# RMSNorm: VectorE's share of the squares moved to ScalarE, which reads x through PSUM copies made by TensorE

## Chip, cores and metric

One core of a Trainium2 chip. The metric is the device time of one execution in microseconds (us); smaller is better. Quoted times are medians of several runs with the lowest and highest in brackets. Runs of the slow state (here: over 1.5% longer than the fastest run of the same kernel) are named where there are any and are left out of every ratio.

Names of the engines in the profile: PE is TensorE's matmul, PEld its weight load, DVE is VectorE, ACT is ScalarE, POOL is GpSimd, SP is SyncE. SBUF and PSUM are the two on-chip memories that the kernel uses: its loads land in SBUF, its matmuls write to PSUM.

## The reference

```python
B, S, D = 512, 32, 640            # x: bf16 [512, 32, 640], g: bf16 [640]
def reference(x, g):
    rms = jnp.sqrt((x * x).mean(axis=-1, keepdims=True) + 1e-6)
    return x / rms * g
```

There are 16384 rows of 640 elements, so each of the 128 partitions holds 128 rows. "A row" below is one row on each of the 128 partitions, a 128x640 operand. The kernel works in 19 chunks, c0 to c18, of 2, 4, 4, fourteen times 8, 4 and 2 rows.

## The kernel before

For each chunk: one load, the mean square of each row (on ACT or on DVE), one square root on ACT, one reciprocal on DVE, one scaling per row on DVE, one product with g on DVE, one store. The parts that matter:

```python
DVE_SS_EVERY = float(os.environ.get("K_DVE_EVERY", "6"))   # every 6th row's square is DVE's
FRONT = [...  "2,2,2" ...]                                 # DVE squares in c0, c1, c2
IO_BUFS = 6; O_BUFS = 3; NODVE_LAST = 3                    # (defaults, shortened)
# ... (cut: pools, g broadcast by a ones-matmul) ...
    for ci, J in enumerate(sizes):
        x_sb_full = xin_pool.tile([P, JM, D], xf.dtype)
        x_sb = x_sb_full[:, :J, :]
        in_eng.dma_start(out=x_sb, in_=x_v[:, r0:r0 + J, :])
        # ... (cut: n_dve, the number of this chunk's squares that DVE takes; na = J - n_dve)
        for j in range(J):
            if j >= na:
                nc.vector.scalar_tensor_tensor(out=junk_d[:], in0=x_sb[:, j, :], scalar=inv_d,
                    in1=x_sb[:, j, :], op0=ALU.mult, op1=ALU.mult, accum_out=ms[:, j:j + 1])
            else:
                nc.scalar.activation(out=junk_a[:], in_=x_sb[:, j, :], func=ACT.Square,
                    scale=inv_sqrt_d, accum_out=ms[:, j:j + 1])
        # ... (cut: tiles; scale_rows and finish, called one after the other)
            nc.scalar.activation(out=rstd[:, j0:j1], in_=ms[:, j0:j1], func=ACT.Sqrt, ...)
            nc.vector.reciprocal(out=rstd[:, j0:j1], in_=rstd[:, j0:j1])
            for j in range(j0, j1):
                nc.vector.tensor_scalar_mul(out=o_sb[:, j, :], in0=src[:, j, :], scalar1=rstd[:, j:j + 1])
            nc.vector.tensor_tensor(out=o_sb, in0=o_sb, in1=g_bcast(J), op=ALU.mult)
            out_eng.dma_start(out=o_v[:, r0:r0 + J, :], in_=o_sb)   # last three chunks: nc.sync
```

Semaphores, and the order of instructions on each engine, are set by the framework when the program is built; each engine then works through its own queue in that order (ACT's late roots in e_psum_dve6, below, show it).

Of the kernel before, what the change touches and what calls it, by code (L numbers as in the profile page):

```python
# [11 lines left out]
J_MAX = int(os.environ.get("K_J", "8"))  # L12
RAMP = [int(v) for v in os.environ.get("K_RAMP", "2,4").split(",") if v]
DRAMP = [int(v) for v in os.environ.get("K_DRAMP", "4,2").split(",") if v]
DVE_SS_EVERY = float(os.environ.get("K_DVE_EVERY", "6"))
FRONT = [int(v) for v in os.environ.get("K_FRONT", "2,2,2").split(",") if v]
IO_BUFS = int(os.environ.get("K_BUFS", "6"))
O_BUFS = int(os.environ.get("K_OBUFS", "3"))
S_BUFS = int(os.environ.get("K_SBUFS", "4"))
OUT_ENG = os.environ.get("K_OUTENG", "gpsimd")  # L20
IN_ENG = os.environ.get("K_INENG", "sync")
G_ENG = os.environ.get("K_GENG", "sync")
G_AFTER = int(os.environ.get("K_GAFTER", "0"))
WARM_SQRT = int(os.environ.get("K_WARM", "1"))
SPLIT = int(os.environ.get("K_SPLIT", "0"))
LAG = int(os.environ.get("K_LAG", "1"))
TTFIRST = int(os.environ.get("K_TTFIRST", "0"))
NODVE_LAST = int(os.environ.get("K_NODVE_LAST", "3"))
LASTOUT_SYNC = int(os.environ.get("K_LASTOUT_SYNC", "3"))
NOLAG_LAST = int(os.environ.get("K_NOLAG_LAST", "0"))  # L30


def chunk_schedule(R):
    start = list(RAMP)
    end = list(DRAMP)
    rem = R - sum(start) - sum(end)
    assert rem >= 0
    mid = []
    while rem >= J_MAX:
        mid.append(J_MAX)  # L40
        rem -= J_MAX
    if rem:
        mid = [rem] + mid
    sizes = start + mid + end
    assert sum(sizes) == R
    return sizes
# [3 lines left out]
def kernel(  # L50
# [6 lines left out]
    nc = tc.nc  # L57
    P = nc.NUM_PARTITIONS
    ALU = mybir.AluOpType
    ACT = mybir.ActivationFunctionType  # L60
    f32 = mybir.dt.float32
# [2 lines left out]
    xf = x.flatten_outer_dims()  # L64
    of = out.flatten_outer_dims()
    N, D = xf.shape
    assert N % P == 0
    R = N // P

    x_v = xf.rearrange("(p r) d -> p r d", p=P)  # L70
# [1 line left out]

    sizes = chunk_schedule(R)
    JM = max(sizes)

    consts = ctx.enter_context(tc.tile_pool(name="consts", bufs=1))
    xin_pool = ctx.enter_context(tc.tile_pool(name="xin", bufs=IO_BUFS))
    out_pool = ctx.enter_context(tc.tile_pool(name="xout", bufs=O_BUFS))
    junk_pool = ctx.enter_context(tc.tile_pool(name="junk", bufs=2))
    small = ctx.enter_context(tc.tile_pool(name="small", bufs=S_BUFS))  # L80
    PACC = int(os.environ.get("K_PACC", "0"))
    if PACC:
        pacc_pool = ctx.enter_context(tc.tile_pool(name="pacc", bufs=PACC, space=bass.MemoryType.PSUM))
    PJUNK = int(os.environ.get("K_PJUNK", "0"))
    if PJUNK:
        pjunk_pool = ctx.enter_context(tc.tile_pool(name="pjunk", bufs=PJUNK, space=bass.MemoryType.PSUM))

    engines = {"sync": nc.sync, "scalar": nc.scalar, "gpsimd": nc.gpsimd, "vector": nc.vector}
    in_eng = engines[IN_ENG]
    out_eng = engines[OUT_ENG]  # L90

    eps_sb = consts.tile([P, 1], f32)
    nc.vector.memset(eps_sb[:], EPS)  # L93
# [4 lines left out]
        warm2 = consts.tile([P, 1], f32)  # L98
        nc.scalar.activation(out=warm2[:], in_=warm[:], func=ACT.Sqrt, bias=eps_sb[:], scale=1.0)  # L99

    GBC = os.environ.get("K_GBC", "pe_act")
    g_sb = consts.tile([P, D], g.dtype)
    g_src = bass.AP(tensor=g.tensor, offset=g.offset, ap=[[0, P], g.ap[-1]])
    if GBC == "dma":
        if not G_AFTER:
            engines[G_ENG].dma_start(out=g_sb[:], in_=g_src)
    else:
        g1 = consts.tile([1, D], g.dtype)
        g_row = bass.AP(tensor=g.tensor, offset=g.offset, ap=[[0, 1], g.ap[-1]])
        engines[G_ENG].dma_start(out=g1[:], in_=g_row)  # L110
        ones1 = consts.tile([1, P], bf16)
        nc.vector.memset(ones1[:], 1.0)  # L112
        gps_pool = ctx.enter_context(tc.tile_pool(name="gps", bufs=1, space=bass.MemoryType.PSUM))
        half = D // 2
        for h in range(2):
            gp = gps_pool.tile([P, half], f32, name=f"gp{h}")
            nc.tensor.matmul(out=gp[:], lhsT=ones1[:], rhs=g1[:, h * half:(h + 1) * half],  # L117
                             start=True, stop=True)
            if GBC == "pe_act":
                nc.scalar.copy(out=g_sb[:, h * half:(h + 1) * half], in_=gp[:])  # L120
            else:
                nc.vector.tensor_copy(out=g_sb[:, h * half:(h + 1) * half], in_=gp[:])

    inv_sqrt_d = 1.0 / float(D) ** 0.5
    inv_d = 1.0 / float(D)

    def g_bcast(J):
        return bass.AP(tensor=g_sb.tensor, offset=g_sb.offset,
                       ap=[list(g_sb.ap[0]), [0, J], list(g_sb.ap[-1])])

    gidx = 0
    r0 = 0
    pending = []
    for ci, J in enumerate(sizes):
        x_sb_full = xin_pool.tile([P, JM, D], xf.dtype)
        x_sb = x_sb_full[:, :J, :]
        in_eng.dma_start(out=x_sb, in_=x_v[:, r0:r0 + J, :])
        if G_AFTER and ci == 0:
            engines[G_ENG].dma_start(out=g_sb[:], in_=g_src)

        if ci < len(FRONT):
            n_dve = min(J, FRONT[ci])
        elif NODVE_LAST and ci >= len(sizes) - NODVE_LAST:
            n_dve = 0
        else:
            n_dve = 0
            for j in range(J):
                k = gidx + j
                if DVE_SS_EVERY and (int(k // DVE_SS_EVERY) != int((k + 1) // DVE_SS_EVERY)):
                    n_dve += 1  # L150
        na = J - n_dve

        if PACC:
            ms = pacc_pool.tile([P, JM], f32)
        else:
            ms = small.tile([P, JM], f32)
        for j in range(J):
            if j >= na:
                junk_d = junk_pool.tile([P, D], bf16)
                nc.vector.scalar_tensor_tensor(  # L160
                    out=junk_d[:],
                    in0=x_sb[:, j, :],
                    scalar=inv_d,
                    in1=x_sb[:, j, :],
                    op0=ALU.mult,
                    op1=ALU.mult,
                    accum_out=ms[:, j:j + 1],
                )
            else:
                if PJUNK:  # L170
                    junk_a = pjunk_pool.tile([P, D], f32)
                else:
                    junk_a = junk_pool.tile([P, D], bf16)
                nc.scalar.activation(  # L174
                    out=junk_a[:],
                    in_=x_sb[:, j, :],
                    func=ACT.Square,
                    scale=inv_sqrt_d,
                    accum_out=ms[:, j:j + 1],
                )  # L180

        rstd = small.tile([P, JM], f32)
        o_sb_full = out_pool.tile([P, JM, D], of.dtype)
        o_sb = o_sb_full[:, :J, :]
        if TTFIRST:
            nc.vector.tensor_tensor(out=o_sb, in0=x_sb, in1=g_bcast(J), op=ALU.mult)

        def scale_rows(j0, j1, rstd=rstd, ms=ms, x_sb=x_sb, o_sb=o_sb):
            if j1 <= j0:
                return  # L190
            nc.scalar.activation(out=rstd[:, j0:j1], in_=ms[:, j0:j1], func=ACT.Sqrt,  # L191
                                 bias=eps_sb[:], scale=1.0)
            nc.vector.reciprocal(out=rstd[:, j0:j1], in_=rstd[:, j0:j1])  # L193
            for j in range(j0, j1):
                src = o_sb if TTFIRST else x_sb
                nc.vector.tensor_scalar_mul(out=o_sb[:, j, :], in0=src[:, j, :],  # L196
                                            scalar1=rstd[:, j:j + 1])

        def finish(J=J, o_sb=o_sb, r0=r0, ci=ci):
            if not TTFIRST:  # L200
                nc.vector.tensor_tensor(out=o_sb, in0=o_sb, in1=g_bcast(J), op=ALU.mult)  # L201
            if LASTOUT_SYNC and ci >= len(sizes) - LASTOUT_SYNC:
                nc.sync.dma_start(out=o_v[:, r0:r0 + J, :], in_=o_sb)
            else:
                out_eng.dma_start(out=o_v[:, r0:r0 + J, :], in_=o_sb)  # L205

        if SPLIT and 0 < n_dve:
            scale_rows(0, na)

            def tail(J=J, na=na, scale_rows=scale_rows, finish=finish):  # L210
                scale_rows(na, J)
                finish()

            pending.append(tail)
        else:
            scale_rows(0, J)
            if SPLIT:
                pending.append(finish)
            else:
                finish()  # L220
        lag = LAG if ci < len(sizes) - NOLAG_LAST else 0
        while len(pending) > lag:
            pending.pop(0)()

        r0 += J
        gidx += J
    while pending:
        pending.pop(0)()


# [28 lines left out]
```

## Time and profile before

| | before |
|---|---|
| time, us | 113.94 (113.86 to 114.06, 3 runs) |
| span of the profiled run, us | 112.0 |
| DVE busy / ACT busy / PE busy | 92% / 73% / 1% |
| DMA rate while loads and stores both run | about 427 GB/s |

The span is the part of a run that the trace covers; the reported time is some 1.9 us longer. The shares of busy time don't say what limits the end. The prediction shows for that the table of stretches: near the end the DMA share collapses and DVE alone is busy. The page's chain of the work that ended last, by engine, of the kernel before:

```profile
issue 52%; DVE 32%; DMA 7%; POOL 4%; SPq 0%; ACT 0%; POOLq 0%
```

"issue" is time in which an engine waited for nothing that the profile shows. Here most of it lies between 42 and 99 us, in stretches of 5 to 7 us between one store issue of POOL and the next, and the waits say what POOL lacked there: DVE's work (90.4 us in all, in 16 waits). DVE itself waited 3.1 us for x and 1.5 us for roots in the whole run.

### The profile page before, as it was taken

Reading aid. Unit: us, or ns where it says so; the run is one execution under the profiler, and the core shown is the slowest. Engines: PE = TensorE matmul, PEld = TensorE weight load, DVE = VectorE, ACT = ScalarE, POOL = GpSimd, SP = SyncE. Lnnn points to the kernel's source line nnn. Section 1 sums busy time; section 2 is a strip of 40 time slices with the busy share of each in tenths; the row PEclk is TensorE's granted clock in tenths of the full one; section 3 lists DMA queues with packets and bytes.
Section 4 is the critical chain, followed back from the end, with each engine's and each line's share of the span. In section 5 each row is a group of like instructions: output and inputs, shape, how many; then the busy total and the mean of one; then the engine's idle time right before and its main releaser. Section 6 shows DMA issues by size and latency. Waiting matters only on the chain.

```text
span 112.0 us, 604 instructions
## 1 busy us (share of the span) xinstructions
PE 0.7 (1%) x2; PEld 0.2 (0%) x2; DVE 102.5 (92%) x217; ACT 81.8 (73%) x231; POOL 10.5 (9%) x20
## 2 busy tenths in 40 slices
PE   2000000000000000000000000000000000000000
PEld 0000000000000000000000000000000000000000
DVE  0589999999999999999999999999996999999860
ACT  6185997999999999899899897979499970000000
POOL 0002111010010101010101001010101002051000
DMA  1999999999999999999999999999999911907994
GB/s 35 408 446 424 378 422 424 426 425 409 435 428 421 424 432 428 421 439 428 421 435 432 421 435 428 420 439 421 426 424 399 411 73 59 410 0 293 413 395 187
DMA packets 5414, 41.98 MB, mean 375 GB/s; under 512 B 609, under 2 KB 610, under 8 KB 1826
## 3 DMA queue, kind: packets, MB, share of 16 engines
q1 hardware_dynamic: 3170, 23.27, 50.2%
q0 software_dynamic: 2240, 18.68, 39.6%
q14 instruction: 4, 0.03, 0.1%
HBM read 20.97 MB, written 20.97 MB: 374 GB/s over the span
## 4 chain that ended last, share of the span: by engine, by line
issue 52%; DVE 32%; DMA 7%; POOL 4%; SPq 0%; ACT 0%; POOLq 0%
DVE o_sb_full L196 13%; DVE o_sb_full L201 10%; DVE junk_d L160 8%; DMA out_dram<-o_sb_full 4%; POOL out_dram L205 4%; DMA x_sb_full<-in_x_dram 3%; DVE rstd L193 1%; SPq L110 0%; ACT rstd L191 0%; POOLq L205 0%; POOLq L254 0%
## 5 line engine op out<-in xcount | busy, mean ns | idle before, releaser
L174 ACT ACTIVATE junk_a<-x_sb_full 128x640 bf16<-128x640 bf16 x104 | 74.9, 721 | 3.5 <-DMA x_sb_full<-in_x_dram 3.5
L201 DVE TENSOR_TENSOR o_sb_full<-o_sb_full,g_sb 128x5120 bf16<-128x5120 bf16 (+2 forms) x19 | 45.5, 2396 | 0.0
L196 DVE TENSOR_SCALAR o_sb_full<-x_sb_full,rstd 128x640 bf16<-128x640 bf16 x128 | 39.8, 380 | 0.4 <-DVE o_sb_full L196 0.4
L160 DVE SCALAR_TENSOR_TENSOR junk_d<-x_sb_full 128x640 bf16<-128x640 bf16 x24 | 19.1, 803 | 3.1 <-DMA x_sb_full<-in_x_dram 3.1
L174 ACT ACTIVATION_READ_ACCUMULATOR junk_a<-x_sb_full 128x1 f32 x104 | 19.4, 187 | 0.0
L205 POOL DMA_DIRECT2D out_dram<-o_sb_full x16 | 10.3, 645 | 90.4 <-DVE o_sb_full L201 47.1
L191 ACT ACTIVATE rstd<-ms,eps_sb 128x8 f32<-128x8 f32 (+2 forms) x19 | 5.2, 289 | 5.4 <-DVE junk_d L160 5.4
L193 DVE RECIPROCAL rstd<-rstd 128x8 f32<-128x8 f32 (+2 forms) x19 | 3.3, 184 | 1.5 <-ACT rstd L191 1.5
L160 DVE DVE_READ_ACCUMULATOR junk_d<-x_sb_full 128x1 f32 x24 | 1.9, 81 | 0.0
L99 ACT ACT_TABLE_LOAD x1 | 1.3, 1283 | 0.7 <-PEq L243 0.7
L120 ACT CAST g_sb<-gp 128x320 bf16<-128x320 f32 x2 | 0.8, 428 | 0.2 <-PE gp L117 0.2
L93 DVE MEMSET eps_sb<- 128x1 f32 x1 | 0.1, 59 | 0.8 <-PEq L243 0.8
L117 PE MATMUL gp<-g,ones 1*128 1x320 bf16 x2 | 0.7, 442 | 2.1 <-DMA g<-in_g_dram 2.1
L99 ACT ACTIVATE warm<-warm,eps_sb 128x1 f32<-128x1 f32 x1 | 0.3, 294 | 0.0
L117 PEld LDWEIGHTS <-ones 1*128 1x128 bf16 x2 | 0.2, 99 | 2.0 <-DVE ones L112 1.1
L112 DVE MEMSET ones<- 1x128 bf16 x1 | 0.2, 165 | 0.0
L243 POOL MEMSET const-float32-0.0<- 128x1 f32 x1 | 0.1, 99 | 0.2 <-issue 0.2
L243 POOL MEMSET const-bfloat16-1.0<- 128x1 bf16 x1 | 0.1, 102 | 0.0
L243 POOL MEMSET const-float32-1.0<- 128x1 f32 x1 | 0.1, 99 | 0.0
L243 POOL MEMSET const-uint8-127<- 128x1 uint8 x1 | 0.1, 99 | 0.0
L97 DVE MEMSET warm<- 128x1 f32 x1 | 0.1, 59 | 0.0
## 6 DMA issues: line engine op xcount, KB each, us to landing
x_sb_full<-in_x_dram SPq DMA_DIRECT2D x14, 1280.0 KB, 16.4
out_dram<-o_sb_full POOLq DMA_DIRECT2D x13, 1280.0 KB, 10.9
x_sb_full<-in_x_dram SPq DMA_DIRECT2D x3, 640.0 KB, 5.3
out_dram<-o_sb_full POOLq DMA_DIRECT2D x2, 640.0 KB, 10.2
out_dram<-o_sb_full SPq DMA_DIRECT2D x1, 1280.0 KB, 4.5
x_sb_full<-in_x_dram SPq DMA_DIRECT2D x2, 320.0 KB, 7.3
out_dram<-o_sb_full SPq DMA_DIRECT2D x1, 640.0 KB, 3.0
out_dram<-o_sb_full POOLq DMA_DIRECT2D x1, 320.0 KB, 7.4
```

What stands on the lines that cost most here:

```text
L99: nc.scalar.activation(out=warm2[:], in_=warm[:], func=ACT.Sqrt, bias=eps_sb[:], scale=1.0)
L112: nc.vector.memset(ones1[:], 1.0)
L117: nc.tensor.matmul(out=gp[:], lhsT=ones1[:], rhs=g1[:, h * half:(h + 1) * half], start=True, stop=True)
L120: nc.scalar.copy(out=g_sb[:, h * half:(h + 1) * half], in_=gp[:])
L160: nc.vector.scalar_tensor_tensor(out=junk_d[:], in0=x_sb[:, j, :], scalar=inv_d, in1=x_sb[:, j, :], op0=ALU.mult, op1=ALU.mult, accum_out= ...
L174: nc.scalar.activation(out=junk_a[:], in_=x_sb[:, j, :], func=ACT.Square, scale=inv_sqrt_d, accum_out=ms[:, j:j + 1],)
L191: nc.scalar.activation(out=rstd[:, j0:j1], in_=ms[:, j0:j1], func=ACT.Sqrt, bias=eps_sb[:], scale=1.0)
L193: nc.vector.reciprocal(out=rstd[:, j0:j1], in_=rstd[:, j0:j1])
L196: nc.vector.tensor_scalar_mul(out=o_sb[:, j, :], in0=src[:, j, :], scalar1=rstd[:, j:j + 1])
L201: nc.vector.tensor_tensor(out=o_sb, in0=o_sb, in1=g_bcast(J), op=ALU.mult)
L205: out_eng.dma_start(out=o_v[:, r0:r0 + J, :], in_=o_sb)
L243: nc = _bacc.Bacc("TRN2", target_bir_lowering=False, num_devices=1)
```

## The change

Its intent is to relieve DVE, the busiest engine. The 18 squares that DVE took in the middle of the run go to ACT. To pay for that, the idle TensorE copies each row that ACT squares into PSUM, as a matmul with an identity, and ACT reads it there, where reading should be cheaper. Besides: three PSUM buffers for the copies, five output buffers for three, eight junk buffers for two, the first two loads are issued before everything else, and g's load moves from SP's queue to ACT's. The lines that act (dead options that were dropped or added are cut):

```diff
-DVE_SS_EVERY = float(os.environ.get("K_DVE_EVERY", "6"))
+DVE_SS_EVERY = float(os.environ.get("K_DVE_EVERY", "0"))
-O_BUFS = int(os.environ.get("K_OBUFS", "3"))
+O_BUFS = int(os.environ.get("K_OBUFS", "5"))
-G_ENG = os.environ.get("K_GENG", "sync")
+G_ENG = os.environ.get("K_GENG", "scalar")
+X0FIRST = int(os.environ.get("K_X0FIRST", "2"))
+XPSUM = int(os.environ.get("K_XPSUM", "3"))
# ... (cut) ...
+    pre_x = {}                       # the first X0FIRST loads, issued before anything else
+    for ci0 in range(min(X0FIRST, nchunks)):
+        ...
+        in_eng.dma_start(out=x_sb_full0[:, :J0, :], in_=x_v[:, r0p:r0p + J0, :])
+    if XPSUM:
+        ident = consts.tile([P, P], bf16, name="ident")
+        make_identity(nc, ident)
+        xps_pool = ctx.enter_context(tc.tile_pool(name="xps", bufs=XPSUM, space=bass.MemoryType.PSUM))
# ... (cut: where ACT's square is emitted) ...
+                if XPSUM:
+                    xp = xps_pool.tile([P, D], f32, name="xp")
+                    c1 = min(512, D)
+                    nc.tensor.matmul(out=xp[:, :c1], lhsT=ident[:], rhs=x_sb[:, j, :c1], start=True, stop=True)
+                    if D > c1:
+                        nc.tensor.matmul(out=xp[:, c1:], lhsT=ident[:], rhs=x_sb[:, j, c1:], start=True, stop=True)
+                    sq_in = xp[:]
                 nc.scalar.activation(
                     out=junk_a[:],
-                    in_=x_sb[:, j, :],
+                    in_=sq_in,
                     func=ACT.Square, ...
```

## The prediction

> **What bounds the kernel now.** I read in this order: the page's busy line, its 40 slices, the table of stretches, the groups, the timeline of one stretch, and ACT's waits. The first two:
>
> ```profile
> PE 0.7 (1%) x2; PEld 0.2 (0%) x2; DVE 102.5 (92%) x217; ACT 81.8 (73%) x231; POOL 10.5 (9%) x20
> ...
> DMA  1999999999999999999999999999999911907994
> GB/s 35 408 446 424 378 422 424 426 425 409 435 428 421 424 432 428 421 439 428 421 435 432 421 435 428 420 439 421 426 424 399 411 73 59 410 0 293 413 395 187
> ```
>
> Two resources look full: the DMA engines in slices 1 to 31 (about 427 GB/s), and DVE nearly to the end. The table of stretches (us; then busy time of PE, PEld, DVE, ACT, POOL; PEclk, DMA share, GB/s) tells which one sets the end:
>
> ```profile
> 70.00:80.00 10.00, 0.00 (x0) 0.00 (x0) 9.76 (x17) 8.27 (x24) 0.53 (x1) 1.00 1.01 428
> 80.00:88.00 8.00, 0.00 (x0) 0.00 (x0) 7.11 (x16) 7.50 (x22) 1.06 (x2) 1.00 0.98 409
> 88.00:94.00 6.00, 0.00 (x0) 0.00 (x0) 6.00 (x14) 3.62 (x12) 0.37 (x1) 1.00 0.35 147
> 94.00:100.00 6.00, 0.00 (x0) 0.00 (x0) 6.00 (x13) 0.00 (x0) 1.02 (x2) 1.00 0.53 218
> 100.00:106.00 6.00, 0.00 (x0) 0.00 (x0) 5.64 (x13) 0.00 (x0) 1.17 (x1) 1.00 0.72 300
> ```
>
> From 88 us on the DMA share falls to a third, ACT stops at about 91, and DVE works alone to 108.4. All input has landed by then; five output chunks (30 of 128 rows) are still to be made. Call the 19 chunks c0 to c18 (2, 4, 4, fourteen of 8, 4, 2 rows). DVE runs 4 to 5 chunks behind the loads, and the tail is DVE paying off that debt. The groups give the prices:
>
> ```profile
> L174 ACT ACTIVATE junk_a<-x_sb_full 128x640 bf16<-128x640 bf16 x104 | 74.9, 721 | 3.5 <-DMA x_sb_full<-in_x_dram 3.5
> L201 DVE TENSOR_TENSOR o_sb_full<-o_sb_full,g_sb 128x5120 bf16<-128x5120 bf16 (+2 forms) x19 | 45.5, 2396 | 0.0
> L196 DVE TENSOR_SCALAR o_sb_full<-x_sb_full,rstd 128x640 bf16<-128x640 bf16 x128 | 39.8, 380 | 0.4 <-DVE o_sb_full L196 0.4
> L160 DVE SCALAR_TENSOR_TENSOR junk_d<-x_sb_full 128x640 bf16<-128x640 bf16 x24 | 19.1, 803 | 3.1 <-DMA x_sb_full<-in_x_dram 3.1
> L120 ACT CAST g_sb<-gp 128x320 bf16<-128x320 f32 x2 | 0.8, 428 | 0.2 <-PE gp L117 0.2
> ```
>
> Successive instructions overlap, so I take spacings from the timeline:
>
> ```profile
> 48.24 0.77 DVE L160 SCALAR_TENSOR_TENSOR junk_d<-x_sb_full 128x640 bf16<-128x640 bf16 x1
> ...
> 48.94 2.45 DVE L196 TENSOR_SCALAR o_sb_full<-x_sb_full,rstd 128x640 bf16<-128x640 bf16 x8
> ...
> 51.30 0.81 DVE L160 SCALAR_TENSOR_TENSOR junk_d<-x_sb_full 128x640 bf16<-128x640 bf16 x1
> ...
> 52.05 2.81 DVE L201 TENSOR_TENSOR o_sb_full<-o_sb_full,g_sb 128x5120 bf16<-128x5120 bf16 x1
> ...
> 54.79 0.19 DVE L193 RECIPROCAL rstd<-rstd 128x8 f32<-128x8 f32 x1
> ```
>
> Eight scalings end 2.4 us after they began, the product with g takes 2.73 (52.05 to 54.79), the reciprocal 0.11, a DVE square 0.75. An 8-row chunk costs DVE 5.25 us plus on average 1.33 squares: 6.25 us. The DMA engines need 8 rows in and 8 out, 2.62 MB at 427 GB/s: 6.14 us. So DVE never catches up on its early lag. ACT does, and starves:
>
> ```profile
> 62.22 0.74 ACT L174 ACTIVATE junk_a<-x_sb_full 128x640 bf16<-128x640 bf16 x1 [0.46 <-DMA x_sb_full<-in_x_dram]
> 68.32 0.74 ACT L174 ACTIVATE junk_a<-x_sb_full 128x640 bf16<-128x640 bf16 x1 [0.76 <-DMA x_sb_full<-in_x_dram]
> 74.41 0.74 ACT L174 ACTIVATE junk_a<-x_sb_full 128x640 bf16<-128x640 bf16 x1 [0.76 <-DMA x_sb_full<-in_x_dram]
> 80.50 0.74 ACT L174 ACTIVATE junk_a<-x_sb_full 128x640 bf16<-128x640 bf16 x1 [1.47 <-DMA x_sb_full<-in_x_dram]
> ```
>
> Fourteen squares follow 80.50, so that is c16 landing, and chunks arrive every 6.1 us, the DMA pace.
>
> **What the Trainium skill says.** (1) "Perfetto Trace Analysis", Optimizing Scalar/DVE Operations: an access overhead per instruction of about 93 ns for ScalarE on SBUF, about 51 ns on PSUM. (2) "VectorE: DVE Perf Modes", the TRN2 errata section: ScalarE takes 224 + N cycles from SBUF, 172 + N from PSUM, at 1.2 GHz. The trace agrees: (224+640)/1.2 = 720 ns against 721; the two casts from PSUM span 0.75 us, each 428 ns, so they start 0.32 us apart, and 320 x 0.833 + 51 = 318. (3) "TensorE: Matmul & The Clock Gate", Parts 1 and 2: matmuls follow each other every N/1.2 ns cold and N/2.4 ns warm, warm after some 3.4 us of steady work; a weight load takes 128/1.2 = 107 ns. Only the cold case is in the trace (weight load 99 ns, isolated N = 320 matmul 442 ns). (4) "DMA: Bandwidth & Descriptors", Queues, rings and completion order: each DMA engine goes round-robin between its queues. The trace fits: loads and stores both move at one chunk per 6.1 us while both have work.
>
> **The change, part by part.** The instruction order says what the diff doesn't: the lag and split code was inert (SPLIT was 0), and PAIR is 0, so neither matters.
>
> *DVE squares.* DVE_SS_EVERY becomes 0: the 24 squares on DVE fall to the 6 of FRONT. 18 x 0.75 = 13.5 us leave DVE; its chunk falls from 6.25 to 5.25 us. They also no longer stand in DVE's queue waiting for later chunks.
>
> *ACT squares from PSUM.* ACT takes 122 rows instead of 104. From SBUF a row repeats every 0.72 us; from PSUM I take 0.72 - 0.093 + 0.051 = 0.677. A chunk costs ACT 8 x 0.677 + 0.19 (square root) = 5.61 us: slower than DVE, faster than the 6.14 of the DMA.
>
> *TensorE.* 122 copies of a row by the identity: matmuls of 512 and 128 columns, two weight loads. Warm: 213 + 53 + up to 214 = at most 480 ns; cold: 534 to 748. Three buffers let it run ahead, so warm it hides.
>
> *Start.* The first load goes out at the head of SP instead of behind g's: 1.14 to about 0.74, worth 0.4 us. Output buffers, 3 to 5: with three, the scaling of a chunk waits for the store three before. Output chunks now come every 5.6 us while stores drain every 6.1, so stores queue; I put the stall avoided at about 1.5 us. Eight junk buffers: nothing.
>
> *The sum along ACT.* ACT reaches c3 when it lands, about 9.6 (18 rows, 2.95 MB, behind a first byte at 2.2, plus 0.5 completion). Then 118 rows x 0.677 = 79.9 and 17 roots x 0.19 = 3.2: the last root ends at 92.7, say 93. DVE is near: c16's root comes 3.9 earlier at 89.2, its output 5.6 later at 94.9, then c17 and c18 (five scalings 1.53, product 1.41, one scaling 0.3, product 0.75, two reciprocals 0.2): 99.1. The last store took 2.6 us to land before and the span ended 1.0 later; with 0.3 for queueing behind c17's store: 103.0. The reported time lay 1.9 above the span (113.94 against 112.0): 104.9.
>
> *The floor from the DMA.* 41.98 MB at 428 GB/s is 98.1 us; from 2.2 that is 100.3; with 0.7 to confirm, 1.0 to the end and 1.9 outside: 103.9.
>
> The two lie one microsecond apart, so both must be nearly perfect. I add 0.4 for TensorE's cold start and waits on the critical engine: 105.3, that is 0.924 of before.
>
> **Rivals.** *A, ACT pays SBUF's price or a bit less* ([...]a wait for PE per row). Each 10 ns of a row is 1.2 us. At 0.70 the time is 107.7; at 0.72, no gain from PSUM at all, 110.1. For: the only PSUM read I have is a cast of 320. Against: it fits to 2 ns.
>
> *B, TensorE becomes the bound.* If it stays cold with exposed weight loads, a row takes 0.748 and the end is 118 x 0.07 = 8.4 us later, 113.5: the whole gain gone. For: warm, it is busy only about half the time, and the trace has no warm matmul. Against: a cold PE that lags is busy without pause, which should warm it; a mixture costs 1 to 3 us.
>
> *C, loads become the bound:* outputs made earlier take their half of the DMA earlier. Against: both queues already share from about 15 us on, so c16 lands again near 80 to 82, and ACT wants it at 83. If c16 lands 2 us late, the time is about 106.
>
> *D, the tail stays with DVE.* It needs 5.25 against ACT's 5.61, so it would have to be slowed by something new. It would show as DVE working on after 101.
>
> **Range and chances.** The base case is 105.3; nothing gets below the DMA's 103.9 by much. Upwards, A and B stretch: 80% within 103.6 to 109.2. Within 2% means over 111.66, which takes a cold TensorE or ACT at over 0.73 a row: 7%. Slower needs another failure: 2%.
>
> **What will show it.** Right: ACT squares 0.677 us apart (recorded mean about 0.69, as 0.428 - 0.267 + 0.533), ACT busy above 95% from 10 to 92 us; DVE idle for some 0.3 us a chunk, waiting for the root; the DMA share at 9 in slices up to about 33, without the hole at 88 to 100; ACT's last root near 93, the last store issued near 99; TensorE mostly under 0.5 us of work a row. Wrong: squares at 720 (A); ACT waiting for PE in the waits, with 512-column matmuls near 430 ns (B); TensorE, and behind it ACT, waiting for x_sb_full before 75 us (C); stores held up by DVE past 101 (D).

## The result

The changed kernel takes 106.48 us (106.39 to 107.44, 11 runs); beside it, in the same rounds, the kernel before took 113.93 (113.63 to 114.07, 14 runs). The ratio is 0.937, 95% interval 0.935 to 0.939. Ratios here are the mean time of one kernel's fast runs over that of the other's of the same rounds, so not quite the ratio of the medians. Three of the 11 runs lie at 107.2 to 107.4; why is open, and below I read the profiled run at 106.48's level (span 104.7). One candidate, not shown: the first loads differ from run to run. TensorE's first copy of c3 begins at 10.15 us in that run, but at 11.53, 11.71 and 11.60 in the profiled runs of e_obuf3, e_psum_dve6 and e_dve6_x10 below, and each of these was the slowest of its kind.

The page of the changed kernel, busy times and two rows of the 40 slices:

```profile
PE 65.4 (62%) x246; PEld 26.5 (25%) x246; DVE 93.0 (89%) x181; ACT 89.9 (86%) x267; POOL 9.8 (9%) x22
...
PEclk9999999998555699999599999755999955795555
DMA  2999999999999999999999999999999999996794
```

DVE's busy time fell by 9.5 us, and it is still the busiest by share. The DMA engines now stay full through slice 35, about 94 us, where before the hole began at about 90. The table of stretches for the end (columns as in the prediction: stretch, length, busy time of PE, PEld, DVE, ACT, POOL, granted clock, DMA share, GB/s):

```profile
80.00:88.00 8.00, 6.20 (x23) 2.46 (x22) 7.78 (x19) 8.00 (x26) 1.12 (x2) 0.72 1.01 420
88.00:94.00 6.00, 4.15 (x16) 1.58 (x14) 5.79 (x12) 6.00 (x21) 0.56 (x1) 0.78 1.02 431
94.00:100.00 6.00, 0.00 (x0) 0.00 (x0) 5.99 (x10) 1.15 (x4) 0.00 (x0) 0.50 0.71 295
```

From 88 to 94 us the DMA share was 0.35 before and is 1.02 now, and ACT, which had stopped at 91, is busy until 95. And the chain that ended last, by engine:

```profile
ACT 72%; DVE 8%; DMA 8%; issue 6%; SPq 1%; PE 1%; ACTq 0%
```

The path has moved from DVE's queue to ACT's. The groups (line, engine, operation, operands, count | busy us, mean ns | idle us before it and what ended it):

```profile
L209 ACT ACTIVATE junk_a<-xp 128x640 bf16<-128x640 f32 x122 | 86.3, 1043 | 2.0 <-PE xp L203 1.9
L200 PE MATMUL xp<-x_sb_full,ident 128*128 128x512 bf16 x122 | 56.0, 463 | 25.7 <-ACT junk_a L209 20.6
```

ACT waited only 1.9 us for its copies in the whole run. PE waited 20.6 us for ACT to give a PSUM buffer back: TensorE follows ACT, not the other way. The mean of 1043 ns for a square needs care. 122 squares of 1043 ns would be 127 us, longer than the run. These records overlap, as the timeline of the changed kernel shows (start, duration; one PE line, then ACT's squares, early and late in the run; ACTIVATION_READ_ACCUMULATOR is the second half of a square, the read of its sum):

```profile
10.15 0.61 PE L200 MATMUL xp<-x_sb_full,ident 128*128 128x512 bf16 x1 [1.89 <-DMA x_sb_full<-in_x_dram]
...
10.90 0.70 ACT L209 ACTIVATE junk_a<-xp 128x640 bf16<-128x640 f32 x1 [1.48 <-PE xp L203]
...
11.78 0.69 ACT L209 ACTIVATE junk_a<-xp 128x640 bf16<-128x640 f32 x1
12.37 0.20 ACT L209 ACTIVATION_READ_ACCUMULATOR junk_a<-xp 128x1 f32 x1
12.46 0.70 ACT L209 ACTIVATE junk_a<-xp 128x640 bf16<-128x640 f32 x1
...
83.39 1.23 ACT L209 ACTIVATE junk_a<-xp 128x640 bf16<-128x640 f32 x1
...
84.06 1.24 ACT L209 ACTIVATE junk_a<-xp 128x640 bf16<-128x640 f32 x1
```

Starts are 0.67 to 0.68 us apart, but each record is a little longer than the one before, 0.70 us at the start and 1.24 at 84 us: the recorded ends drift away from the recorded starts. A row is two instructions: the read of the sum starts 0.58 to 0.59 us after the square, and the next square 0.09 after that, 0.677 together (median of the starts). In the kernel before the two steps are 0.63 and 0.09 (squares at 39.33 and 40.05, the read at 39.96). What others see of ACT is the end. DVE's reciprocals, one per 8-row chunk, wait for ACT's root, and give its true pace:

```profile
17.58 0.20 DVE L233 RECIPROCAL rstd<-rstd 128x8 f32<-128x8 f32 x1 [1.50 <-ACT rstd L231]
...
85.61 0.20 DVE L233 RECIPROCAL rstd<-rstd 128x8 f32<-128x8 f32 x1
...
91.28 0.20 DVE L233 RECIPROCAL rstd<-rstd 128x8 f32<-128x8 f32 x1
...
100.26 0.83 DVE L145 TENSOR_TENSOR o_sb_full<-o_sb_full,g_sb 128x1280 bf16<-128x1280 bf16 x1
```

There are twelve chunks between 17.58 and 85.61: 68.03 / 12 = 5.67 us each. Less 0.19 for the root, a square takes 5.48 / 8 = 0.685 us. TensorE's copies, which wait for ACT to free a buffer, also begin 0.685 us apart. The last line is the last product; it ends at 101.09, and only the last store follows.

### The profile page after: what moved, and what is told of

Same layout as the page of the kernel before. It is cut to its first block, busy times and chain, and to the rows that moved or that the text cites. A ratio compares the mean times of both kernels' runs of the same rounds, so it can differ in the third digit from the quotient of the medians.

```text
span 104.7 us, 1104 instructions
## 1 busy us (share of the span) xinstructions
PE 65.4 (62%) x246; PEld 26.5 (25%) x246; DVE 93.0 (89%) x181; ACT 89.9 (86%) x267; POOL 9.8 (9%) x22
## 4 chain that ended last, share of the span: by engine, by line
ACT 72%; DVE 8%; DMA 8%; issue 6%; SPq 1%; PE 1%; ACTq 0%
ACT junk_a L209 70%; DMA x_sb_full<-in_x_dram 8%; DVE o_sb_full L143 4%; DVE o_sb_full L145 3%; ACT rstd L231 3%; SPq L92 1%; PE xp L200 1%; DVE rstd L233 0%; SPq L159 0%; PE xp L203 0%; ACTq L231 0%
## 5 line engine op out<-in xcount | busy, mean ns | idle before, releaser
L209 ACT ACTIVATE junk_a<-xp 128x640 bf16<-128x640 f32 x122 | 86.3, 1043 | 2.0 <-PE xp L203 1.9
L200 PE MATMUL xp<-x_sb_full,ident 128*128 128x512 bf16 x122 | 56.0, 463 | 25.7 <-ACT junk_a L209 20.6
L209 ACT ACTIVATION_READ_ACCUMULATOR junk_a<-xp 128x1 f32 x122 | 65.5, 549 | 0.0
L203 PE MATMUL xp<-x_sb_full,ident 128*128 128x128 bf16 x122 | 31.4, 257 | 0.0
L203 PEld LDWEIGHTS <-ident 128*128 128x128 bf16 x122 | 12.3, 101 | 39.4 <-issue 39.4
L200 PEld LDWEIGHTS <-ident 128*128 128x128 bf16 x122 | 14.3, 118 | 24.8 <-issue 13.9
L149 POOL DMA_DIRECT2D out_dram<-o_sb_full x16 | 9.1, 571 | 81.6 <-DVE o_sb_full L145 77.9
L231 ACT ACTIVATE rstd<-ms,eps_sb 128x8 f32<-128x8 f32 (+2 forms) x19 | 11.2, 589 | 2.0 <-DVE junk_d L187 2.0
L187 DVE SCALAR_TENSOR_TENSOR junk_d<-x_sb_full 128x640 bf16<-128x640 bf16 x6 | 4.8, 817 | 2.8 <-DMA x_sb_full<-in_x_dram 2.8
L187 DVE DVE_READ_ACCUMULATOR junk_d<-x_sb_full 128x1 f32 x6 | 0.5, 82 | 0.0
## 6 DMA issues: line engine op xcount, KB each, us to landing
x_sb_full<-in_x_dram SPq DMA_DIRECT2D x2, 320.0 KB, 10.9
```

Of the source, the lines that this page charges most:

```text
L200: nc.tensor.matmul(out=xp[:, :c1], lhsT=ident[:], rhs=x_sb[:, j, :c1], start=True, stop=True)
L203: nc.tensor.matmul(out=xp[:, c1:], lhsT=ident[:], rhs=x_sb[:, j, c1:], start=True, stop=True)
L209: nc.scalar.activation(out=junk_a[:], in_=sq_in, func=ACT.Square, scale=inv_sqrt_d, accum_out=ms[:, moff + j:moff + j + 1],)
L231: nc.scalar.activation(out=rstd[:, :J], in_=ms[:, :J], func=ACT.Sqrt, bias=eps_sb[:], scale=1.0)
```

## The experiments

My theory after this result: the kernel before ends when DVE has paid its debt; the changed kernel ends when ACT has got through its queue of 118 rows from c3 on, at 0.685 us a row. Then half the gain should come without PSUM. Each experiment is the changed kernel (or, where said, the kernel before) with the default of one or two settings edited.

### Parts of the change taken alone

**e_nopsum: no PSUM copies.** `-XPSUM ... "3"` / `+XPSUM ... "0"`

> The changed kernel with the squares reading x from SBUF again (no copy through TensorE and PSUM); all else as changed. Theory (ACT's queue of squares is the path from 11 to 95 us): a row goes back from 0.685 us (spacing in the changed kernel) to 0.72 us; 118 rows x 0.035 = 4.1 us later, less the 0.75 us that the first PE copy of chunk 3 took: about 109.9 us. Rival 1 (the gain is DVE's alone, ACT has slack): no change, 106.5. Rival 2 (PE's copies and their waits cost as much as PSUM saves): 106 or less.

Measured: 110.16 us (109.86 to 110.35), ratio to before 0.965 (0.961 to 0.969).

**e_before_nodve: the kernel before, with DVE's squares in the middle moved to ACT.** `-DVE_SS_EVERY ... "6"` / `+DVE_SS_EVERY ... "0"`

> The kernel before with one number changed: no squares on DVE after the front (18 rows moved from DVE to ACT). Nothing through PSUM, three output buffers, g loaded first. Theory: DVE's debt goes, but ACT at 0.72 us a row becomes the path: as the run without PSUM, 109.9, plus 0.4 for the later first load, plus 0 to 1 for three output buffers: 110.3 to 111.3, so about 3 us of the 7.4 gained. Rival (PSUM is what makes the change work at all): 113 to 114.

Measured: 110.29 us (110.19 to 110.38), ratio 0.967 (0.964 to 0.969).

The two agree within their spread: without PSUM the rest of the change (start, five output buffers, junk buffers) is worth about nothing (the eight junk buffers were not taken alone together with PSUM; what they are worth there is open), and moving 18 squares off DVE is worth 3.6 us, although ACT gets them at the full SBUF price. The timeline of the changed kernel without PSUM shows the bound:

```profile
41.62 0.20 DVE L233 RECIPROCAL rstd<-rstd 128x8 f32<-128x8 f32 x1 [0.38 <-ACT rstd L231]
...
47.57 0.20 DVE L233 RECIPROCAL rstd<-rstd 128x8 f32<-128x8 f32 x1 [0.39 <-ACT rstd L231]
```

One chunk takes 5.95 us = 8 x 0.72 + 0.19, and DVE waits 0.4 us for each root: ACT is the bound there too. So PSUM's share of the gain is the remaining 110.2 to 106.5 = 3.7 us. The pace alone accounts for 118 x (0.72 - 0.685) = 4.1. The copy that ACT waits for when c3 lands (0.75, from PE's 10.15 to ACT's 10.90 above) should take a part of that back, but the two traces don't show it: in the profiled run without PSUM c3 landed later, and ACT's first square of it starts at 11.05.

**e_start: the old order of the first loads.** `-X0FIRST ... "2"`, `-G_ENG ... "scalar"` / `+X0FIRST ... "0"`, `+G_ENG ... "sync"`

> The changed kernel with the old start: g loaded first on SP, then the loads of x. Theory: the first load goes out 0.4 us later, chunk 3 lands 0.4 us later, ACT's chain shifts as a whole: 106.9. Rival (the start is hidden behind a later wait): 106.5.

Measured: 106.56 us (106.54 to 107.08), ratio 0.937 (0.934 to 0.939), that of the changed kernel. The rival is right. The loads do come 0.3 us later, but ACT's second square of c3 starts at 11.88 us against 11.78: with the later loads c2's root ran ahead of c3's first square instead of behind it, inside a wait that ACT had anyway.

**e_obuf3: three output buffers again.** `-O_BUFS ... "5"` / `+O_BUFS ... "3"`

> The changed kernel with three output buffers in place of five. Theory: the scaling of a chunk then waits for the store three before, which the changed kernel's stores (landing 11 to 15 us after issue) reach later than the 11.3 us that three periods of 5.67 less the chunk's own 5.7 allow: DVE held up by 1 to 2 us in all, 107.5 to 108.5. Rival: the stores land sooner when fewer are out, and nothing changes: 106.5.

Measured: 109.55 us (109.43 to 111.0), ratio 0.963 (0.957 to 0.970). The direction is as expected, the size is not: 3.1 us, not 1 to 2. The profiled run was its slowest (111.0); DVE's timeline there:

```profile
55.21 2.46 DVE L143 TENSOR_SCALAR o_sb_full<-x_sb_full,rstd 128x640 bf16<-128x640 bf16 x8 [0.68 <-DVE rstd L233]
...
61.32 2.46 DVE L143 TENSOR_SCALAR o_sb_full<-x_sb_full,rstd 128x640 bf16<-128x640 bf16 x8 [0.68 <-DVE rstd L233]
```

DVE idles 0.68 us in front of the scalings although its own reciprocal, named as the releaser, ended well before; in one other chunk the profile names the store. Chunks are 6.11 us apart, which is the pace of the DMA engines and not ACT's 5.67, although ACT's roots in this run still come every 5.67: the stores now hold DVE. (c3 lands 1.4 us late in this profiled run, about as much as the run lies above the median.) Without PSUM chunks come only every 5.95 us, and e_before_nodve (three buffers) and e_nopsum (five) don't differ: in the trace of e_before_nodve DVE was held in front of its scalings once, for 0.1 us. So the buffers have a value only together with the faster ACT, and are then most of what PSUM gains.

### Is 0.685 us ACT's own pace?

**e_static: all squares read one and the same PSUM tile; TensorE makes only the first copy.** Its output is wrong, which doesn't matter for the time.

```diff
+        xp_once = []
-                if XPSUM:
+                if XPSUM and xp_once:
+                    sq_in = xp_once[0][:]
+                elif XPSUM:
                     xp = xps_pool.tile([P, D], f32, name="xp")
+                    xp_once.append(xp)
```

> Wrong result on purpose: one row is copied into PSUM once, and all 122 squares on ACT read that same PSUM tile, so nothing waits for TensorE copies. It measures the pace of a square from PSUM by itself. Theory 1 (0.685 us is ACT's own pace from PSUM): squares still end 0.685 us apart and the recorded durations grow in the same way. Theory 2 (0.677 is ACT's own pace, and the ring of three PSUM tiles with TensorE's copy adds 0.008): squares end 0.676 to 0.678 apart. The time itself says little, since ACT also starts earlier: 104 to 106.5.

Measured: 105.55 us in one look. The reciprocals there:

```profile
44.67 0.20 DVE L237 RECIPROCAL rstd<-rstd 128x8 f32<-128x8 f32 x1
...
50.34 0.20 DVE L237 RECIPROCAL rstd<-rstd 128x8 f32<-128x8 f32 x1
```

5.67 us a chunk without any copy or any wait for TensorE, and the recorded durations grow in the same way (1.06 us at 43.3, 1.13 at 49.8). So 0.685 is ACT's own price for this square with accumulation from PSUM. What TensorE costs beyond it is at most the 0.9 us by which this one run is shorter (its squares don't wait for loads of x either).

**e_bufs4: four PSUM buffers.** To make room, g is broadcast by a DMA instead of a matmul: `-XPSUM ... "3"`, `-GBC ... "pe_act"` / `+XPSUM ... "4"`, `+GBC ... "dma"`

> The changed kernel with four PSUM tiles in place of three; to make room g is spread over the partitions by its DMA, not by TensorE. Theory (ACT's own pace): no change, 106.2 to 106.8, TensorE still waiting for ACT in the waits. Rival (the ring of three tiles sets the pace): a row falls to 0.677, 118 x 0.008 = 0.9 us less, 105.6.

Measured: 109.1 us (109.05 to 109.13), ratio 0.958 (0.956 to 0.959), outside both expectations. The side edit explains it. The 0.16 MB of the broadcast moved beside the first loads and landed 6.0 us after its issue: slice 1 moved 181 GB/s instead of 423, and DVE's first wait for x was 5.7 us instead of 2.8. In the middle ACT's pace is that of three buffers. The run says that the ring of three isn't the limit; as a measure of the buffers' worth in time it is spoiled.

### DVE's squares kept, with PSUM

**e_psum_dve6: PSUM copies, but every sixth square stays on DVE.** `-DVE_SS_EVERY ... "0"` / `+DVE_SS_EVERY ... "6"`

> The changed kernel with the DVE squares back (every sixth row), squares on ACT still from PSUM. Theory: DVE is the path again at 6.25 us a chunk or a little more, since its instructions now depend on each other more closely: 113.0 to 114.0, the whole gain gone although PSUM makes ACT faster still. Rival (PSUM source is the gain): about 106 to 107.

Measured: 118.9 us (118.48 to 120.34, one of four runs slow, which the median includes), ratio of the fast runs 1.041 (1.037 to 1.046): slower than the kernel before, and a clear miss. (The fast runs alone have a median of 118.59.) I had expected DVE's debt to set the time as before.

**e_dve6_x10: the same with ten input buffers for six.** `-IO_BUFS ... "6"` / `+IO_BUFS ... "10"`

> Why did the changed kernel with the DVE squares back take 118.9 and not 113 to 114? The same kernel with ten input buffers in place of six. Theory: with every sixth row on DVE, a chunk's root stands in ACT's queue behind squares of later chunks; those wait for loads, which wait for a buffer that only DVE's scaling of an earlier chunk frees: a loop that six buffers tighten. With ten, loads come early, and DVE's own 6.25 us a chunk is left: 112.5 to 114.5. Rival (DVE or PE instructions themselves cost more in this mix): about 118 to 119 again.

Measured: 118.87 us (118.42 to 120.15), ratio 1.045 (1.043 to 1.048). My first explanation, a loop through the input buffers, falls.

**e_nopsum_dve6: DVE's squares kept, no PSUM.** `-DVE_SS_EVERY ... "0"`, `-XPSUM ... "3"` / `+DVE_SS_EVERY ... "6"`, `+XPSUM ... "0"`

> The changed kernel with every sixth square back on VectorE and the squares of ScalarE back on the SBUF copy of x: all that is left of the change is the new order of the start and the five output buffers. It tells whose fault the 118.9 us of the changed kernel with VectorE's squares is. Theory (the step to PSUM, with the order in which it makes ScalarE take squares and roots, causes the loss): as the kernel before, 113.3 to 114.3 us, ratio 0.995 to 1.003. Rival (the other parts of the changed kernel cause it when VectorE has squares): 117 to 119 us.

Measured: 113.62 us (113.40 to 116.12, the last of these slow and in the median; 113.44 for the fast runs), ratio 0.9985 (0.995 to 1.002): as before. So it is the step to PSUM that costs 5.2 us when DVE keeps its squares, and gains 3.7 when it doesn't:

| median of the fast runs, us | x from SBUF | x from PSUM |
|---|---|---|
| every 6th square on DVE | 113.4 | 118.6 |
| none in the middle | 110.2 | 106.5 |

All four have the new start and five output buffers. The waits (engine, line, what it waited for: us in total, times, longest) of the version with PSUM and then of the one without it:

```profile
ACT junk_a L209 <- PE xp L203: 11.4, 10, 1.6
...
DVE rstd L233 <- ACT rstd L231: 6.9, 6, 2.9
```

```profile
DVE rstd L233 <- ACT rstd L231: 1.7, 3, 0.9
```

DVE waits 5.2 us longer for roots, the size of the loss (the profiled run with PSUM was the slow one, 120.34; in e_dve6_x10's, which counts as fast, the wait is 6.8). Why the roots are late can be read in ACT's timeline, with DVE's reciprocal after it:

```profile
68.58 0.74 ACT L209 ACTIVATE junk_a<-xp 128x640 bf16<-128x640 f32 x1
...
70.85 0.70 ACT L209 ACTIVATE junk_a<-xp 128x640 bf16<-128x640 f32 x1 [1.44 <-PE xp L203]
...
71.54 0.70 ACT L209 ACTIVATE junk_a<-xp 128x640 bf16<-128x640 f32 x1
...
72.22 0.30 ACT L231 ACTIVATE rstd<-ms,eps_sb 128x8 f32<-128x8 f32 x1
```

```profile
72.55 0.20 DVE L233 RECIPROCAL rstd<-rstd 128x8 f32<-128x8 f32 x1 [2.88 <-ACT rstd L231]
```

Counting ACT's instructions from the start, this root is c11's, and stands behind 79 squares; c11 and all before it have only 64 on ACT. The two squares in front of it are c14's, three chunks on, and waited for c14's load. DVE stood idle for 2.88 us for a root that lacked nothing but its turn. Without PSUM the same root stands behind 73 squares, the last three of them c13's. In the changed kernel itself, without DVE's squares, each root from c2 on to c16 stands one square behind its own chunk, and this can't happen. So with DVE's squares ACT's built order is the fault, and the PSUM version's is worse by up to six squares. That the order is all of it I have read, not shown: no run changed the order alone.

### What is left at the two ends

**e_front: DVE's two squares of c2 go to c3.** In the changed kernel ACT idles from 9.4 to 10.9 us (the 1.48 above), while c2 has only two squares for it. `-FRONT ... "2,2,2"` / `+FRONT ... "2,2,0,2"`

> One half of the attempt to beat both: only the front is moved (chunk 2's two DVE squares to ACT, two of chunk 3 to DVE), the end stays 8, 4, 2. Theory: ACT idles less near 10 us and its whole chain shifts by 0.7 to 1.4 us: 105.1 to 105.8. Rival (what was gained came from the smaller last chunks): 106.4 to 106.6.

Measured: 105.56 us (105.44 to 105.62), ratio to before 0.928 (0.926 to 0.929), the best version. ACT no longer idles there, and DVE's last reciprocals start 1.4 us earlier, at 95.32 against 96.75, which is two squares at 0.685. The time gains 0.9. DVE is close behind ACT here: its reciprocals from 17.27 to 44.60 come every 5.47 us without a wait for a root, and only later every 5.67. The stretch from 94 to 100 us suggests where the other half went:

```profile
94.00:100.00 6.00, 0.00 (x0) 0.00 (x0) 5.62 (x11) 0.00 (x0) 0.00 (x0) 0.50 0.92 385
```

The DMA share there is 0.92, against 0.71 in the changed kernel: the bytes are running out of room. No run tests this.

**e_ends: e_front, and one more chunk at the end, of 6 rows, so that the tail is 6, 4, 2.** (By the rule that makes the chunks, c2 grows from 4 rows to 6, and there are thirteen chunks of 8 for fourteen.) `-DRAMP ... "4,2"` / `+DRAMP ... "6,4,2"`

> An attempt to beat both: the two squares of chunk 2 that DVE did go to ACT, which stood idle there, and DVE takes two of chunk 3 instead; chunks at the end shrink as 8, 6, 4, 2 in place of 8, 4, 2 and chunk 2 has 6 rows. Theory: ACT idles 1.5 us less near 10 us (last root near 93.7 in place of 95), and DVE, left with 2 rows instead of the rest of 14 after it, ends 4 us sooner; then the DMA engines are the bound at 103.9: 104.0 to 104.8. Rival (the DVE tail is hidden behind the stores anyway): 105.5 to 106.5.

Measured: 105.84 us (105.61 to 106.63), ratio 0.931 (0.926 to 0.935): the rival's range; the gain over the changed kernel was less than expected, and none over e_front.

**e_ends_x8: the same with eight input buffers.** `-IO_BUFS ... "6"` / `+IO_BUFS ... "8"`

> The attempt with both ends moved, and eight input buffers in place of six. In it ACT waited 1.3 us in all for late loads and the last load landed at 92.3. Theory: earlier loads take those waits away and let the last chunks reach DVE sooner, so the DMA engines stay full to the end: 104.8 to 105.4. Rival (the DMA engines were full anyway, and loads that come sooner only make stores come later): 105.6 to 106.0.

Measured: 105.76 us (105.63 to 106.71), ratio 0.931 (0.928 to 0.934). The time is the rival's. The DMA share in the profiled run, the slowest, was 1.01 from 80 to 88 us, 0.98 to 94 and 0.89 to 100, so there was little room for earlier input to use.

## Why the prediction was right, and where it was off

The time was 106.48 against 105.3 predicted, inside the range. The mechanism held: DVE's debt goes, ACT's queue sets the end, the DMA engines come close behind. The terms of the sum, each against the trace:

| step | predicted | measured | adds, us |
|---|---|---|---|
| ACT's first square of c3 | 9.6 | 10.90 | +1.3 |
| ACT's pace, per row | 0.677 | 0.685 (113 rows to c16's root: 0.9, less what rounding 92.7 up to 93 had added) | +0.8 |
| c16's root to its finished product | 5.6 | 5.56 (91.28 to 96.84) | 0 |
| end of the last product | 99.1 | 101.09 | (sum of the above) |
| last product to the end of the span | 3.9 | 3.6 | -0.3 |
| outside the span | 1.9 | 1.8 | -0.1 |
| margin for TensorE and for waits | 0.4 | its copy is in the first line | -0.4 |

The sum without the margin was 104.9. The terms give 104.9 + 1.3 + 0.8 - 0.3 - 0.1 = 106.6, measured 106.5.

- **The c3 term was mis-sized by 1.3 us.** The chain began at the landing of c3. It left out that ACT can't begin before TensorE has copied the first row, 0.75 us with the clock at half; the rest is a landing some 0.5 later. The 0.4 set aside for TensorE covered half of that copy. The trace at hand already gave the landing: in the kernel before, the last semaphore update of c3's load is at 10.40, and the first load goes out 0.4 earlier now (10.10 in the changed kernel).
- **ACT's pace was mis-sized by 8 ns a row.** The 42 ns between SBUF and PSUM were right to the nanosecond for the starts: up to about 56 us squares start 0.677 apart. Their ends, which DVE and TensorE wait for, come 0.685 apart. e_static shows that this is ACT itself, not TensorE behind it. Two of the checks in the prediction were weaker than they look. The cast that fits to 2 ns fits the 51 ns; the table's 172 cycles would give it 410 ns, and its record has 428. And the 720 of the table meet the length of a record (721), while the spacing of 0.72 is the sum of the square's 0.63 and the 0.09 of the read of its sum, which the prediction doesn't mention. So rival A (ACT pays part of the SBUF price) was a fifth right: 8 of the 43 ns.
- **Rival B, TensorE as the bound: not so, for a reason the prediction didn't have.** Its clock does stay low for much of the run (the PEclk row: stretches at 5). But even at half clock it keeps up: from 26 to 35 us the granted clock is 0.50, and copies begin every 0.685 us there as elsewhere. How fast they could come shows early in the run, where ACT holds nothing up (the clock's records begin only at 15.3 us, but 512 columns take 0.63 us there, as against 0.58 in the stretches at 0.50 and 0.38 at full clock). These copies begin

```profile
10.66 0.63 PE L200 MATMUL xp<-x_sb_full,ident 128*128 128x512 bf16 x1
...
11.19 0.63 PE L200 MATMUL xp<-x_sb_full,ident 128*128 128x512 bf16 x1
```

  0.53 us apart, which is less than ACT's 0.685. I had allowed up to 0.748 cold, with both weight loads exposed; they are hidden.
- **Rival C, loads as the bound: no.** TensorE waited for x three times, 5.0 us in all, every time before 11 us. Loads matter only in the versions that keep DVE's squares and PSUM.
- **Rival D, a tail on DVE: no,** though DVE ended its last product at 101.09, past my mark of 101. It followed ACT one root at a time; its tail from c16's root took what was predicted for it.
- **The start, 0.4: worth nothing** (e_start). Time given to a load isn't time given to the path, when the engine behind it has other work to shift into the wait.
- **Output buffers, 1.5: 3.1** (e_obuf3). I counted stalls of single chunks. In the run the stores' pace of 6.1 us takes over from ACT's 5.67 chunk after chunk.
- **The floor of 103.9 from the DMA engines** stands: the best version, at 105.56, is 1.7 above it.

Small slips in the prediction: thirteen squares follow the one at 80.50, fourteen with it; rival A's 107.7 and 110.1 are counted from 104.9 and not from 105.3; and the 13.5 us that were to leave DVE are 9.5 in its busy time.

Of what I said would show it: ACT was busy 29.1 of the 30 us from 10 to 40, and without a gap from 40 to 94, as expected. A recorded mean near 0.69 us was wrong (1043 ns), since records stretch. The last root was expected near 93; its record starts at 94.89. The hole in the DMA share at 88 to 100 did not go: it moved to 94 and is shallower. And DVE was to idle 0.3 us a chunk; it waited 0.11 for each root. Its own pace is 5.47 us (e_front), not 5.25: where each of its instructions waits for the one before, they overlap less. So a faster ACT would have gained 0.2 us a chunk before DVE set the pace again.

## What to carry to other kernels

When the busiest engine is relieved, price the next one's queue from the first instruction it can run to its last, at its own spacing: here that gave 110 us without PSUM and 105 with it before any run, both within 1.5%. A cheaper operand source pays only as far as the buffers behind it allow (three output buffers gave back 3.1 of 3.7 us), and a half-done version can lose: with DVE's squares left in place the same PSUM copies made the kernel 4% slower. When reading recorded durations, check that count times mean fits in the span; if not, take the pace from whoever waits for that engine.

## What the Trainium skill lacked or had wrong

- "VectorE: DVE Perf Modes", the TRN2 errata section: 172 + 640 cycles are 0.677 us for 640 elements from PSUM on ScalarE. The pace of the square with accumulation was 0.685 us (5.67 us per chunk of eight and a root), also with nothing written to PSUM meanwhile. That is 1% of a row, but 1 us in this kernel.
- No page that I read prices the read of the accumulator on ScalarE: the next square starts 0.09 us after it, from SBUF and from PSUM alike. The square before it takes 0.626 and 0.584 us; their difference is the 42 ns between the access overheads that "Perfetto Trace Analysis", Optimizing Scalar/DVE Operations, gives for ScalarE.
- "Perfetto Trace Analysis", the per-instruction lifecycle: nothing there prepares for records of one form of instruction that grow from 0.70 to 1.24 us over a run while the engine's pace stays at 0.685. I found no cause. A wait of ACT sets the length back (in e_psum_dve6 above, 0.74 at 68.58, and 0.70 at 70.85 after a wait of 1.44), so it looks like ends that fall behind the starts. From SBUF the same squares kept a mean of 0.72.
- "TensorE: Matmul & The Clock Gate", Part 2, says that the spacing of a stream of weight load and matmul pairs is set by both, pipelined. Here the pipelining hid the loads wholly: a 640-column copy with two weight loads repeated every 0.53 us in the early copies shown above, which is 640 columns at the 1.2 GHz that the page gives for the cold clock. One pair of copies shows it.
- No page that I read says what a small transfer beside the first loads costs them: with the 0.16 MB broadcast of g, DVE's first wait for x grew by 2.9 us and the time by 2.6 (e_bufs4).
